# Another order of TensorE's 950 units in a fused talking-heads attention and squared-ReLU FFN

## The chip, the cores and the metric

The kernel runs on one core of one Trainium2 chip. The metric is the time of one execution in device microseconds.

## What is computed

Eight batches of attention with 12 heads, 448 positions and 64 elements a head, in which the heads are mixed before and after the softmax, and then an FFN with a squared ReLU over the 3584 tokens:

```python
scale = 1.0 / np.sqrt(q.shape[-1])
scores = scale * np.matmul(q, k.transpose(0, 1, 3, 2))
scores = np.einsum('bhij,hg->bgij', scores, w_pre)
scores = scores - np.max(scores, axis=-1, keepdims=True)
attn = np.exp(scores)
attn = attn / (np.sum(attn, axis=-1, keepdims=True) + 1e-09)
attn = np.einsum('bhij,hg->bgij', attn, w_post)
x = np.matmul(attn, v)            # (8, 12, 448, 64), as tokens (3584, 768)
h = np.maximum(x @ w_in, 0.0)     # (3584, 2048)
out = h * h @ w_out               # (3584, 768)
```

Inputs and output are float32. The kernel works in bfloat16 with float32 sums in PSUM.

## The kernel before

The whole kernel is a list of tasks that a planner lays out when the program is built. Nothing is decided on the chip: each engine gets a fixed list, and semaphores order the lists against each other.

TensorE's work is cut into units, each a run of matmuls that is issued without a break. The units form ten streams, and within a stream their order is fixed:

- **T** (L841 in batch 0, L847 after): transposes of q and k.
- **QK** (L1087): the scores of one tile of query rows, for two heads a unit or, in the last tile of 64 rows, four. Each score tile is copied to `stage` by ACT or DVE (L486, L487), and SP's DMAs then lay it out anew in `dring` (the relayout, L1134), 10 query rows to a slot, so that heads stand on partitions.
- **pre** (L1162, L1170, L1177): the head mixing before the softmax, two slots of `dring` at a time. ACT takes the exponential into `pring` (L1215), DVE the reciprocal of the sums into `rinv` (L1231), POOL folds it into the second mixing matrix, `wk2s` (L1239), and DVE or POOL multiplies the last columns, `ptail` (L1250).
- **post** (L1287): the head mixing after the softmax, 14 matmuls to a unit, evicted to `a2t` by ACT or DVE.
- **AV** (L1349): attention times values, evicted to `xt`.
- **direct** (L985, L1006, L1028): scores and first mixing of batch 0 without a relayout.
- **F1** (two streams; L1401 in batches 0 and 1, L1427 after): the first FFN product, with ReLU on ACT or DVE (L1460, L1461) and the square on DVE (L1470) into `h2t`.
- **F2** (two streams; L1555, and L1498 for the last two tiles): the second FFN product, evicted to `osb` and stored.

`ORDER`, a string of 950 characters, says from which stream the next unit is taken. A digit is a stream: 0 is T, 1 QK, 2 pre, 3 post, 4 AV, 5 direct, 6 and 7 F1, 8 and 9 F2. Three letters are a stream too, but with another tiling mode of TensorE's array. The units run in modes: *full* (128 x 128), *row* (two halves of 64 rows side by side), *cols* (two halves of 64 columns) and *quad* (four quadrants of 64 x 64). A digit 2 is a pre unit in quadrants, `a` one in row mode and `b` one in column mode; `c` is a QK unit that takes row mode where it could be in quadrants. That choice is there only for the last query tile of a batch, 64 rows; for other QK units `c` and `1` are the same.

```python
STREAM = {"a": 2, "b": 2, "c": 1, **{str(i): i for i in range(10)}}
...
t_qk.alts = {"c": ("row", 2 * 189.2 + 8.0)}
...
t_pre.alts = {"a": ("row", held), "b": ("cols", 2 * 189.2 + 8.0)}
```

The planner goes through `ORDER` in `_Plan.run`, with a cost for each task. It deals the eight PSUM banks out to the units, the oldest free ones first, and gives each task that may run on either of two engines (`FLEX`: most evictions) to the one that would end it first by its costs. So another order also changes which bank a unit gets, which engine evicts it and in which order ACT, DVE and POOL work. `warm_up` puts in extra matmuls (L659) where the plan has long gaps early on.

A unit starts on the chip when its inputs are there and its banks have been evicted. If one waits, all units behind it in TensorE's list wait too.

Of the kernel before, what the change touches and what calls it, by code (L numbers as in the profile page):

```python
# [28 lines left out]
INF = float("inf")  # L29
STREAM = {"a": 2, "b": 2, "c": 1, **{str(i): i for i in range(10)}}  # L30
ORDER = (
    "00c0c0011055cc555555515551551555555155532525b3b350515c2355025aabb5533a00b0a502a3ac33c33b"
    "2144bcb4c2c3b376732263633762272366a773c633336724cc7144cac26377122763676633236c7722c76673"
    "c9cc392239a9338a00381218b44138334200200c27a81a18c1c83338c33662c167c2267731a67276c3336722"
    "2444213773c66613c76721633001672236722712676381183a8223830072830308c3a8c11822393191339c11"
    "932244229c19a393339ca23244224433a6336c37cc7aa006c163a73c72261167373a63362170037224382200"
    "83a18311811912293392239c83338a38c118c3c4222444423361a16a17c373c61a6303072372161267337326"
    "216a7003734b422009cc913191319c381a382228382293393a39c3c931142224441c83c82228c8336136337a"
    "c722006326227337612167337621637100722009c393cc9c3392228c83a182238813c8a3381c8c3342244224"
    "44223761c716363a63731176c006337221762236733700a8381218382229c92239030931931c9c3c931c9222"  # L40
    "4442c83a383c831381224442227637a6c6c731617c6c36337212762236733378212818333822244422933922"
    "29393383683382287637767a6676733864447667766776678766776789989988988999"
)


# [1792 lines left out]
```

## Time and profile before

| | |
|---|---|
| median of 3 runs | 525.28 us (523.45 to 525.76) |
| profiled execution, its own time | 523.65 us |
| its span | 521.9 us |
| PE busy | 507.9 us (97%) |
| ACT busy | 451.9 us (87%) |
| DVE busy | 436.2 us (84%) |
| POOL busy | 209.5 us (40%) |
| chain that ended last | PE 69%, ACT 19%, DMA 5%, DVE 4% |
| granted TensorE clock | 1.00 |

PE is TensorE's matmuls and PEld its weight loads, which overlap them. The span runs from the first to the last instruction; the execution's own time has 1.75 us around it. Busy shares are averages over stages with different limits, and since matmuls are pipelined, a busy PE is not one at its peak. The chain that ended last is followed back from the last instruction, at each step to what released it.

### The profile page before, as it was taken

How to read it: one execution, taken by the hardware profiler on the slowest of the kernel's cores; microseconds unless marked ns; L12 is line 12 of the kernel's file. 1: busy time of each engine (PE TensorE's matmuls, PEld its weight loads, DVE VectorE, ACT ScalarE, POOL GpSimd, SP SyncE). 2: the span in 40 equal slices, each digit the busy share in tenths (PEclk: the TensorE clock that was granted, in tenths of full speed). 3: DMA queues.
4: the chain of work that ended last, by engine and by line, in shares of the span. 5: the costliest groups of instructions: out<-in, count | busy, mean ns of one | idle time of the engine just before them, and what ended most of it. 6: DMA issues, size and time to landing. Idle time of an engine off the chain costs nothing.

```text
span 521.9 us, 22053 instructions
## 1 busy us (share of the span) xinstructions
PE 507.9 (97%) x8925; PEld 318.8 (61%) x8925; DVE 436.2 (84%) x1213; ACT 451.9 (87%) x1286; POOL 209.5 (40%) x413
## 2 busy tenths in 40 slices
PE   7899999999999999999999999999999999999997
PEld 4344677667856665557546565567555665568974
DVE  8799888889999899988998879988998868976530
ACT  5899998999999899989999999988899898996411
POOL 9405545333464374135532377024633341243010
PEclk9999999999999999999999999999999999999999
DMA  9999999756895599647983689446985566642014
GB/s 177 201 197 159 201 175 201 163 118 133 156 181 139 124 168 171 123 104 168 174 161 62 150 166 200 98 90 152 174 131 117 119 151 121 117 87 64 3 24 103
DMA packets 82518, 72.07 MB, mean 138 GB/s; under 512 B 13502, under 2 KB 79662, under 8 KB 82414
## 3 DMA queue, kind: packets, MB, share of 16 engines
q0 software_dynamic: 36480, 32.58, 39.1%
q1 hardware_dynamic: 45514, 37.83, 30.1%
q8 instruction: 73, 1.20, 0.9%
q10 hardware_dynamic: 420, 0.20, 0.2%
q14 instruction: 31, 0.25, 0.1%
HBM read 45.70 MB, written 11.01 MB: 109 GB/s over the span
## 4 chain that ended last, share of the span: by engine, by line
PE 69%; ACT 19%; DMA 5%; DVE 4%; issue 1%; POOL 1%; SPq 1%; ACTq 0%; DVEq 0%
PE ps L1555 24%; PE ps L1427 16%; ACT pring L1215 8%; PE ps L1349 6%; PE ps L1287 5%; PE ps L1087 5%; ACT stage L486 5%; PE ps L1177 4%; ACT a2t L486 3%; PE ps L1498 2%; PE ps L1401 2%; PE ps L1162 2%; DVE stage L487 2%; ACT h1t L1460 2%; DMA dring<-stage 1%
## 5 line engine op out<-in xcount | busy, mean ns | idle before, releaser
L1215 ACT ACTIVATE pring<-ps 128x448 bf16<-128x448 f32 (+1 forms) x368 | 196.8, 568 | 6.4 <-PE ps L1177 4.6
L1239 POOL TENSOR_TENSOR wk2s<-wk2b,rinv 128x120 bf16<-128x120 bf16 x179 | 73.6, 414 | 208.4 <-DVE rinv L1231 207.0
L1555 PE MATMUL ps<-w_out_sb,h2t 64*128 64x384 bf16 x1664 | 151.8, 323 | 0.1
L487 DVE CAST a2t<-ps 128x420 bf16<-128x420 f32 x202 | 126.3, 655 | 11.2 <-PE ps L1287 10.2
L1427 PE MATMUL ps<-xt,w_in_sb 64*128 64x448 bf16 (+2 forms) x1344 | 122.5, 322 | 0.6 <-ACT stage L486 0.2
L486 ACT ACTIVATE stage<-ps 128x448 bf16<-128x448 f32 (+1 forms) x206 | 106.8, 558 | 10.3 <-PE ps L1087 9.2
L1555 PEld LDWEIGHTS ps<-w_out_sb,h2t 64*128 64x128 bf16 x1664 | 79.2, 94 | 49.3 <-issue 1.5
L486 ACT ACTIVATE a2t<-ps 128x420 bf16<-128x420 f32 x158 | 98.3, 673 | 7.8 <-PE ps L1287 7.4
L487 DVE CAST stage<-ps 128x448 bf16<-128x448 f32 (+1 forms) x154 | 92.2, 616 | 10.5 <-PE ps L1087 8.9
L1427 PEld LDWEIGHTS ps<-xt,w_in_sb 64*128 64x128 bf16 x1344 | 62.7, 94 | 40.7 <-PE ps L1177 1.2
L1215 ACT ACTIVATION_READ_ACCUMULATOR pring<-ps 128x1 f32 (+1 forms) x368 | 85.7, 233 | 0.0
L1590 POOL DMA_DIRECT2D out_dram<-osb x52 | 33.6, 652 | 86.9 <-DVE osb L487 34.2
L1287 PEld LDWEIGHTS ps<-wk2s,pring 60*128 60x128 bf16 x2160 | 52.1, 93 | 26.2 <-ACT pring L1215 2.5
L1287 PE MATMUL ps<-wk2s,pring 60*128 60x60 bf16 x2160 | 61.1, 188 | 3.1 <-issue 1.1
L1087 PE MATMUL ps<-qkt 64*128 64x448 bf16 (+1 forms) x360 | 52.9, 354 | 3.1 <-DVE w_out_sb L948 1.3
L1460 ACT ACTIVATE h1t<-ps 128x448 bf16<-128x448 f32 (+2 forms) x92 | 41.2, 459 | 15.5 <-PE ps L1427 12.6
L1470 DVE TENSOR_TENSOR h2t<-h1t 128x448 bf16<-128x448 bf16 (+2 forms) x176 | 50.9, 322 | 1.9 <-ACT h1t L1460 1.7
L1250 DVE TENSOR_TENSOR ptail<-pring,rinv 128x128 bf16<-128x128 bf16 x161 | 48.2, 299 | 1.3
L1461 DVE TENSOR_SCALAR h1t<-ps 128x448 bf16<-128x448 f32 (+2 forms) x84 | 41.0, 489 | 9.4 <-PE ps L1427 6.5
L1231 DVE RECIPROCAL rinv<-sums 128x2 f32<-128x2 f32 x184 | 28.9, 157 | 18.2 <-ACT pring L1215 17.3
L1401 PE MATMUL ps<-xt,w_in_sb 128*128 128x228 bf16 (+1 forms) x384 | 42.5, 260 | 0.0
L1177 PE MATMUL ps<-dring,wk1r 64*64 64x448 bf16 (+1 forms) x540 | 41.2, 363 | 0.3 <-DMA dring<-stage 0.3
(87 smaller groups left out, 596.4 us busy)
## 6 DMA issues: line engine op xcount, KB each, us to landing
dring<-stage SPq DMA_DIRECT2D x308, 105.0 KB
out_dram<-osb POOLq DMA_DIRECT2D x52, 192.0 KB, 3.8
qraw<-in_q_dram POOLq DMA_DIRECT2D x42, 112.0 KB, 5.4
kraw<-in_k_dram POOLq DMA_DIRECT2D x42, 112.0 KB, 5.6
w_in_sb<-in_moe_w_in_dram POOLq DMA_DIRECT2D x8, 384.0 KB, 11.1
vraw<-in_v_dram POOLq DMA_DIRECT2D x24, 128.0 KB, 5.0
w_out_sb<-in_moe_w_out_dram POOLq DMA_DIRECT2D x8, 384.0 KB, 9.0
vraw<-in_v_dram POOLq DMA_DIRECT2D x24, 96.0 KB, 5.7
```

The costliest lines, as they stand in the source:

```text
L486: return eng.activation(o, i_, AF.Copy)
L487: return eng.tensor_copy(o, i_)
L1087: r_ = eng.matmul(ps[o:o + i_, g.banks[x], 0:S], qkt[r0:r0 + 64, pb, p_ % 3, 0, p_ // 3, i0 + w - i_:i0 + w], qkt[r0:r0 + 64, pb, p_ % 3, ...
L1177: r_ = eng.matmul(ps[64 * y:64 * y + 64, gr.banks[x], 0:S], wk1[64 * x:64 * x + 64 - R0 * x, :], dring[64 * x:64 * x + 64 - R0 * x, (g0 + ...
L1215: return eng.activation(pring[0:r1, pr, 0:S], ps[0:r1, gr.banks[x], 0:S], AF.Exp, accum_out=sums[0:r1, g, :], **bias)
L1239: return eng.tensor_tensor(wk2s[:, p0:p0 + n, :], i0.to_broadcast([128, n, PR]), rinv[:, p0:p0 + n, :].to_broadcast([128, n, PR]), ALU.mult)
L1287: r_ = eng.matmul(ps[:, gr.banks[x], o * PR:(o + 1) * PR], p_, w_, start=True, stop=True)
L1401: r_ = eng.matmul(ps[:, g.banks[0], 0:n], w_in_sb[:, ft, t * 128:(t + 1) * 128], xt[:, ft, c0:c1], start=(ft == 0), stop=(ft == NFT - 1))
L1427: r_ = eng.matmul(ps[z * m:(z + 1) * m, g.banks[x], 0:n], w_in_sb[64 * y:64 * y + 64, ft, t:t + m], xt[64 * y:64 * y + 64, ft, c0:c1], sta ...
L1460: return eng.activation(h1t[:, s, 0:n], ps[:, g.banks[x], 0:n], AF.Relu)
L1470: return eng.tensor_tensor(h2t[:, t16, o0:o0 + n], h1t[:, s, 0:n], h1t[:, s, 0:n], ALU.mult)
L1555: r_ = eng.matmul(ps[z * m:(z + 1) * m, g.banks[hh], 0:FH], h2t[64 * y:64 * y + 64, t16, col + z * m:col + (z + 1) * m], w_out_sb[64 * y:6 ...
```

## The change

Only the string `ORDER` is another. It is the result of a search for the mean of four planned executions, three of them with random delays of evictions, relayouts and fetches. Its first line and its last, of 11:

```diff
 ORDER = (
-    "00c0c0011055cc555555515551551555555155555525b3b350515c2355025aabb5533a00b0a502a3ac33c33b"
+    "00c0100c1055155c555551555c5515555555c55a52323523505c5c235502a5aba5532300a0a50a23ac333c3a"
     ...
-    "29393383683382287637767a6676733864447667766776678766776789989988988999"
+    "393383382228836376a677663763736784447677676867866776677679989998899988"
 )
```

The streams give the same 950 units. 544 of the 950 places hold the same character. Most units move by few places; the largest moves are 13 places later (a pre unit) and 10 earlier (an F2 unit).

Three places in TensorE's list, before and now. The first is in batch 1, where the pre units (L1177) need the relayout of the batch's second score tile; L1401 is F1 of batch 0, L1287 post, L1087 QK of the third tile. Before:

```order
L1287 MATMUL ps<-wk2s,pring 128x60 x6
L1287 MATMUL ps<-wk2b,ptail 128x60 x2
L1287 MATMUL ps<-wk2s,pring 128x60 x6
L1401 MATMUL ps<-xt,w_in_sb 128x228 x6
L1087 MATMUL ps<-qkt 128x448 x2
L1401 MATMUL ps<-xt,w_in_sb 128x228 x12
L1177 MATMUL ps<-dring,wk1r 64x448 x8
L1087 MATMUL ps<-qkt 128x448 x2
L1401 MATMUL ps<-xt,w_in_sb 128x228 x24
```

And now:

```order
L1087 MATMUL ps<-qkt 128x448 x4
L1401 MATMUL ps<-xt,w_in_sb 128x228 x18
L1287 MATMUL ps<-wk2s,pring 128x60 x6
L1287 MATMUL ps<-wk2b,ptail 128x60 x2
L1287 MATMUL ps<-wk2s,pring 128x60 x6
L1177 MATMUL ps<-dring,wk1r 64x448 x8
L1401 MATMUL ps<-xt,w_in_sb 128x228 x18
```

One QK unit and F1 units have moved ahead of the two pre units (L1177 x8). From the last QK unit of the second tile to these pre units there are 14 F1 units now for 12, three QK units for two, and as many post and pre units as before.

The second place is in batch 5: pre units (L1177 in quadrants, L1162 in row mode) between F1 units of batch 4 (L1427) and post units (L1287). Before:

```order
L1287 MATMUL ps<-wk2s,pring 128x60 x6
L1177 MATMUL ps<-dring,wk1r 64x448 x4
L1427 MATMUL ps<-xt,w_in_sb 128x448 x12
L1177 MATMUL ps<-dring,wk1r 64x448 x8
L1427 MATMUL ps<-xt,w_in_sb 128x448 x12
```

And now:

```order
L1287 MATMUL ps<-wk2s,pring 128x60 x6
L1162 MATMUL ps<-dring,wk1r 128x448 x4
L1427 MATMUL ps<-xt,w_in_sb 128x448 x12
L1287 MATMUL ps<-wk2s,pring 128x60 x6
L1287 MATMUL ps<-wk2b,ptail 128x60 x2
L1287 MATMUL ps<-wk2s,pring 128x60 x6
L1162 MATMUL ps<-dring,wk1r 128x448 x4
L1427 MATMUL ps<-xt,w_in_sb 128x448 x12
```

The pre units stand singly between post and F1 units, and in row mode, as their neighbours are, where one and then two of them stood in quadrants.

The third place is in batch 7, where two pre units of the second score tile are followed later by their post units; L1087 with 64 partitions is QK in quadrants, L1555 is F2 of batch 6. Before:

```order
L1177 MATMUL ps<-dring,wk1r 64x448 x4
L1087 MATMUL ps<-qkt 64x448 x4
L1177 MATMUL ps<-dring,wk1r 64x448 x4
L1555 MATMUL ps<-w_out_sb,h2t 128x384 x16
L1087 MATMUL ps<-qkt 64x448 x4
L1555 MATMUL ps<-w_out_sb,h2t 128x384 x16
L1287 MATMUL ps<-wk2s,pring 128x60 x6
L1287 MATMUL ps<-wk2b,ptail 128x60 x2
L1287 MATMUL ps<-wk2s,pring 128x60 x12
```

And now:

```order
L1177 MATMUL ps<-dring,wk1r 64x448 x8
L1287 MATMUL ps<-wk2s,pring 128x60 x6
L1287 MATMUL ps<-wk2b,ptail 128x60 x2
L1287 MATMUL ps<-wk2s,pring 128x60 x6
L1555 MATMUL ps<-w_out_sb,h2t 128x384 x16
L1087 MATMUL ps<-qkt 128x448 x2
L1087 MATMUL ps<-qkt 64x448 x2
L1287 MATMUL ps<-wk2s,pring 128x60 x6
L1287 MATMUL ps<-wk2b,ptail 128x60 x2
L1287 MATMUL ps<-wk2s,pring 128x60 x6
L1555 MATMUL ps<-w_out_sb,h2t 128x384 x16
```

The two pre units stand together, a post unit has come in behind them, one QK unit has gone to row mode (two matmuls of 128 partitions and two of 64), and the other one, not in these rows any more, stands behind the post units that follow.

SP's list of DMAs has the same rows in both orders. POOL's list has 16 tail products for 23; DVE has 168 for 161.

More of the change, by code (lines that the diff above doesn't have):

```diff
@@ L31 @@
 ORDER = (
[L32 to L41, printed above, removed]
-    "29393383683382287637767a6676733864447667766776678766776789989988988999"
+    "00c0100c1055155c555551555c5515555555c55a52323523505c5c235502a5aba5532300a0a50a23ac333c3a"
+    "b144b1a4c2c3a367732263733662272366a1736333367244c11741a127763162276377673263117663227763"
+    "1913192239a9338a00381244128318334200200c2728ca1811c833381336621c761226773ca6727613337622"
+    "244421377316663c17672173030c67223662272167638118a382238307302800a382238c3813911c9c3393cc"
+    "9c2244229319a193339c2a3244224433a63c6c371c720a06316ca73373a621367c7a63362170037224382200"
+    "8ccc83c181a932293392239183ac8331813813c422b444423363ac61a7cc7cc63a63003723721612673373a6"
+    "262170037342249a0019c1c913c92238338223811822933933a91cc9c3342224442183182238318163363a7c"
+    "17220063a63a73a736126733762116700722009119111933392228183a38322838c383ca8311813c42244422"
+    "44322637163c7631a6731c76313600722176226733700a833821183822293922c90309cc9311913393c19222"
+    "444238a1833383c18c2244422267613776cc6317163a3637c22762236c733782238c38338122444229392229"
+    "393383382228836376a677663763736784447677676867866776677679989998899988"
 )
```

## The prediction

> **What bounds the kernel now.** I read the page's engine lines first, then the busy time by stretch, then TensorE's own waits, then single instructions in order of time at the places where the order changes.
>
> ```profile
> span 521.9 us, 22053 instructions
> PE 507.9 (97%) x8925; PEld 318.8 (61%) x8925; DVE 436.2 (84%) x1213; ACT 451.9 (87%) x1286; POOL 209.5 (40%) x413
> ```
>
> Busy time by stretch (the stretch and its length; then PE, PEld, DVE, ACT and POOL busy; granted clock, DMA share, GB/s):
>
> ```profile
> 16.00:60.00 44.00, 40.98 (x669) 20.80 (x668) 39.13 (x115) 40.82 (x124) 15.72 (x30) 1.00 1.05 185
> 60.00:486.00 426.00, 423.04 (x7628) 268.24 (x7626) 373.02 (x1014) 392.96 (x1122) 176.50 (x350) 1.00 0.70 139
> 486.00:522.00 36.00, 32.20 (x442) 23.78 (x436) 9.90 (x34) 8.51 (x22) 2.53 (x4) 1.00 0.20 47
> ```
>
> PE is idle for 44.00 − 40.98 = 3.02 us between 16 and 60 us, and for 426.00 − 423.04 = 2.96 us in all the time from 60 to 486 us. The granted clock is 1.00 in every stretch. ACT is next, with 392.96 of 426 us. So TensorE's stream sets the end, and an order can change three things in it: how long a unit takes in the tiling mode that the order gives it, how often the mode changes, and the waits. The idle time that can be seen after the start-up is 3.02 + 2.96 = 5.98 us, so that is about all that a better order could win from waits. The longest waits, the first of them still in the start-up (us in total, times, longest):
>
> ```profile
> PE ps L1087 <- DVE w_out_sb L948: 1.3, 1, 1.3
> PE ps L1287 <- issue: 1.1, 1, 1.1
> PE ps L1287 <- DVE ptail L1250: 0.5, 1, 0.5
> PE ps L1177 <- DMA dring<-stage: 0.3, 1, 0.3
> ```
>
> **Modes and mode changes.** The prices are read from TensorE's instructions in order of time (start us, us, form, count). What a group costs is the time from its start to the start of the next row shown below it; its own length is longer, since matmuls are pipelined.
>
> ```profile
> 96.61 0.55 PE L1162 MATMUL ps<-dring,wk1r 64*128 64x448 bf16 x4
> 96.99 0.58 PE L847 MATMUL ps<-ident,qkt 64*128 64x64 bf16 x28
> ...
> 97.59 1.47 PE L1555 MATMUL ps<-w_out_sb,h2t 64*128 64x384 bf16 x16
> 98.99 0.38 PE L1087 MATMUL ps<-qkt 64*64 64x448 bf16 x4
> 99.21 0.36 PE L1177 MATMUL ps<-dring,wk1r 64*64 64x448 bf16 x4
> ...
> 101.28 0.57 PE L1170 MATMUL ps<-dring,wk1c 124*64 124x448 bf16 x4
> 101.69 0.50 PE L1349 MATMUL ps<-a2t,vraw 128*64 128x220 bf16 x8
> ...
> 227.44 0.35 PE L1087 MATMUL ps<-qkt 64*128 64x448 bf16 x2
> 227.73 0.57 PE L1177 MATMUL ps<-dring,wk1r 64*64 64x448 bf16 x8
> 228.23 1.47 PE L1555 MATMUL ps<-w_out_sb,h2t 64*128 64x384 bf16 x16
> 229.54 0.25 PE L1287 MATMUL ps<-wk2s,pring 60*128 60x60 bf16 x6
> ```
>
> An F2 unit of 16 matmuls takes 229.54 − 228.23 = 1.31 us when a unit of the same row mode follows, and 98.99 − 97.59 = 1.40 us when a quadrant unit follows: a change of mode costs 0.09 us. A pre unit takes 96.99 − 96.61 = 0.38 us in row mode, 101.69 − 101.28 = 0.41 us in column mode (a column unit follows), and in quadrant mode (228.23 − 227.73 − 0.09) / 2 = 0.205 us. A QK unit of a batch's last, 64-row tile takes 99.21 − 98.99 = 0.22 us in quadrant mode. For its row mode, which before does not use, two row pairs bound it: 2 × (227.73 − 227.44 − 0.09) = 0.40 us; a second pair hidden wholly would make it 0.22, so nothing is lost or gained below that, and I take 0.40.
>
> Counted in the two orders (954 units in each, four warm-ups among them), the matmuls of pre go from 112 to 132 at L1162, from 24 to 12 at L1170 and from 540 to 532 at L1177: five row units more, three column units and two quadrant units less. That is 5 × 0.38 − 3 × 0.41 − 2 × 0.205 = +0.26 us. Three QK units go from quadrant to row mode: 3 × (0.40 − 0.22) = +0.54 us. Mode changes go from 286 to 284: −0.18 us. All other units are there in the same number and form. Together TensorE's own work grows by 0.62 us.
>
> **The start-up.** The order now puts two direct units (L1028) between the last two QK units of the first tile, where before waited longest.
>
> ```profile
> 15.74 0.37 PE L1087 MATMUL ps<-qkt 64*128 64x448 bf16 x2 [1.26 <-DVE w_out_sb L948]
> 17.36 2.12 PE L1028 MATMUL ps<-qkt,w_out_sb 128*128 128x448 bf16 x10 [0.34 <-ACT stage L486]
> 15.05 0.98 ACT L486 ACTIVATE stage<-ps 128x448 bf16<-128x448 f32 x2
> 16.76 1.85 ACT L486 ACTIVATE stage<-ps 128x448 bf16<-128x448 f32 x4
> ```
>
> It looks like a gain of up to 1.26 us, but I cost it at nothing. By the kernel's own dealing out of banks the QK unit waited for a PSUM bank that the first of the two evictions at 15.05 gives back about 0.5 us later (the trace names a DVE instruction). In the new order the second of the two direct units takes that bank, the QK unit the next one, and the direct unit after them needs, as before, the bank that the first eviction at 16.76 frees. It started at 17.36, and ACT's list of work is the same up to there, so it starts at 17.36 again. The bounds are 0 and −1.26.
>
> **The relayout at 84 us.** Two pre units of batch 1 wait here for the relayout of its second score tile (the first place shown with the change). First the chain that ended last, then TensorE:
>
> ```profile
> 72.26 0.32 PE ps L1087 x2
> 77.03 7.44 DMA dring<-stage
> 84.51 0.38 PE ps L1177 x4
> ```
>
> ```profile
> 82.59 1.34 PE L1401 MATMUL ps<-xt,w_in_sb 128*128 128x228 bf16 x12
> 83.86 0.38 PE L1177 MATMUL ps<-dring,wk1r 64*64 64x448 bf16 x4
> ```
>
> The tile's last QK unit runs at 72.26, the first pre unit at 83.86, and the second waits until 84.51 for its relayout, 0.3 us. In the new order two F1 units (L1401) and one QK unit more stand in between: (83.86 − 82.59) + 0.20 = 1.47 us more cover, against a wait of 0.3 us. It goes: −0.3. If the relayout lands later too, it stays. SP's list of relayouts is the same, so what each is queued behind does not change; POOL's loads keep their order but for one pair of batch 5 and 6.
>
> **The tail products at 456 us.** Here a post unit waits for DVE (the third place shown with the change):
>
> ```profile
> 455.88 0.62 DVE L487 CAST stage<-ps 64x448 bf16<-64x448 f32 x1
> 456.42 0.28 DVE L1250 TENSOR_TENSOR ptail<-pring,rinv 128x128 bf16<-128x128 bf16 x1
> 456.76 0.26 PE L1287 MATMUL ps<-wk2s,pring 60*128 60x60 bf16 x6 [0.54 <-DVE ptail L1250]
> ```
>
> The tail product (L1250) stood behind a score eviction (0.62 us) of the second quadrant QK unit. In the new order that QK unit comes after the post unit, and the work between the pre unit and its post unit is two F2 units as before, one QK unit and one post unit more. The wait goes: −0.54 us. If DVE takes another eviction in its stead, it stays; the bounds are 0 and −0.54.
>
> **The instruction wait.** The wait of 1.1 us put down to "issue" falls inside one post unit at 57 us. The successions of post, pre and F1 around it have the same forms and counts in both orders, so I leave it. The queue of instructions:
>
> ```profile
> q8 instruction: 73, 1.20, 0.9%
> ```
>
> The Trainium skill, "Runtime: NRT & Kernel Launch", section Instruction fetch mechanics, says that an engine's instructions come in blocks of 256 and that crossing a block is mostly hidden. The 73 transfers, one for some 250 of TensorE's instructions, agree with the blocks; that 1.1 us had no other releaser speaks against "hidden" here. By the rule the wait would be an accident and gone, and the sum 1.1 us lower.
>
> **New waits.** I counted in the orders how much TensorE work stands between each unit after 60 us and the nearest unit whose eviction it needs. Less than 1.25 us of cover have 66 units before and 74 now; between 1.25 and 1.5 us it is 93 and 82. If all 2.96 us of idle time after 60 us belonged to the 66, eight more would cost 0.36 us; if none did, nothing. I take +0.4.
>
> **The sum.** +0.62 − 0.3 − 0.54 + 0.4 = +0.2 us. The profiled execution took 523.65 us (span 521.9 and 1.75 around it), so the same kind of execution would take 523.85. It lies 1.63 us below the median of the runs shown, 525.28; on that median the forecast is 525.5 us. Within 0.5% (2.6 us, about what a measurement of this kernel can tell, with runs from 523.45 to 525.76) is no change.
>
> **Rivals.**
>
> *Most waits go (faster).* An order with more slack against late evictions, relayouts and instructions could take two thirds of the 5.98 us: −4.0 + 0.62 = −3.4, so 521.9 us. For it speaks that two of the waits quoted have more cover. Against it: the issue wait, 1.1 of the 5.98 us, stands where the order gives nothing, and short covers have not become fewer. It needs 2.6 + 0.62 = 3.2 us of waits gone before it shows.
>
> *ACT becomes the bound (slower).* The evictions are dealt out between ACT and DVE again with the new order. ACT gets 162 of the evictions to a2t for 158; DVE loses those four and takes seven tail products from POOL. In batch 6 alone five a2t evictions go from DVE to ACT.
>
> ```profile
> L487 DVE CAST a2t<-ps 128x420 bf16<-128x420 f32 x202 | 126.3, 655 | 11.2 <-PE ps L1287 10.2
> L486 ACT ACTIVATE a2t<-ps 128x420 bf16<-128x420 f32 x158 | 98.3, 673 | 7.8 <-PE ps L1287 7.4
> 380.00:420.00 40.00, 39.85 (x748) 24.35 (x742) 36.20 (x91) 36.84 (x102) 13.58 (x28) 1.00 0.61 123
> 420.00:460.00 40.00, 39.30 (x661) 23.19 (x655) 32.38 (x84) 35.48 (x98) 11.59 (x23) 1.00 0.60 121
> ```
>
> The four are 4 × 0.673 = 2.7 us; the smaller kinds, of which ACT gains some and gives some back, I put at +0.8, together 3.5 us. The five of batch 6 are 3.4 us. ACT has 40.00 − 36.84 + 40.00 − 35.48 = 7.68 us of idle time there, which is why I don't expect it. But its exponentials (L1215) can't go to another engine, and each pair of them holds two PSUM banks. If the 3.5 us came in bursts and TensorE had to wait for all of them, the time would be 525.28 + 0.62 + 3.5 = 529.4 us. It decides from the point where more than some 2 of the 3.5 us fall into bursts. The Trainium skill, "TensorEngine Tiling (Array Packing)", section PSUM Bottleneck, says that tiling speeds up TensorE and not the eviction of PSUM, which may then become the bottleneck; ACT's 392.96 of 426 us agrees that it is near, PE's 423.04 that it is not there yet.
>
> **How the numbers follow.** The forecast of no change has 0.55: the terms known are small and of both signs. The faster rival gets 0.20, the slower one 0.25, as work was added for sure and the waits are only thought to go. The range reaches to the slower rival, 529.5, and a little beyond the faster one, 521.5; the forecast's own range is 523 to 528.
>
> **What would show it.** In the profile after, PE should be busy as before within 1 us, with an idle time of 5 to 6.5 us between 16 and 486 us; L1028 should start its row near 17.4 us again; the wait of L1177 for a relayout near 84 us and that of L1287 for ptail near 456 us should be gone; the issue wait near 57 us should still be there. The forecast is wrong if PE's idle time changes by over 3 us, or if the units between two places of the same kind take longer without idle time.

## The result, and the profile after

The changed kernel takes 525.58 us (median of 20 runs, 524.24 to 528.16), the kernel before 523.42 us (20 runs, 522.16 to 525.76). The ratio is 1.0042 (95% interval 1.0027 to 1.0058): 2.2 us or 0.4% slower, under the 0.5% within which the forecast called it no change. The forecast was 525.5 us.

The profiled execution of the changed kernel took 528.16 us, 4.5 us more than the one of before. The page's engine lines:

```profile
span 526.4 us, 22062 instructions
PE 511.6 (97%) x8925; PEld 317.5 (60%) x8925; DVE 437.4 (83%) x1212; ACT 455.1 (86%) x1294; POOL 207.2 (39%) x406
```

Busy time by stretch, columns as in the prediction:

```profile
16.00:60.00 44.00, 40.62 (x661) 20.51 (x660) 40.12 (x119) 40.14 (x122) 15.72 (x30) 1.00 1.06 185
60.00:490.00 430.00, 426.05 (x7621) 266.32 (x7621) 375.02 (x1015) 396.37 (x1130) 174.13 (x343) 1.00 0.69 138
490.00:527.00 37.00, 32.76 (x454) 24.34 (x450) 9.11 (x33) 8.98 (x23) 2.52 (x4) 1.00 0.19 46
```

PE idles for 44.00 − 40.62 = 3.38 us between 16 and 60 us, and for 430.00 − 426.05 = 3.95 us from 60 to 490: 7.33 us, where before had 5.98. Its waits (us in total, times, longest) and the two places of the prediction, TensorE's instructions in order of time:

```profile
PE ps L1287 <- issue: 2.1, 2, 1.9
PE ps L1555 <- issue: 1.0, 1, 1.0
PE ps L1087 <- DVE h1t L1461: 0.3, 1, 0.3
```

```profile
17.33 2.12 PE L1028 MATMUL ps<-qkt,w_out_sb 128*128 128x448 bf16 x10
...
86.93 0.57 PE L1177 MATMUL ps<-dring,wk1r 64*64 64x448 bf16 x8
...
457.54 1.46 PE L1555 MATMUL ps<-w_out_sb,h2t 64*128 64x384 bf16 x16
458.84 0.66 PE L1087 MATMUL ps<-qkt 64*128 64x448 bf16 x4
459.43 0.26 PE L1287 MATMUL ps<-wk2s,pring 60*128 60x60 bf16 x6
```

The start-up ends at 17.33 us (17.36 before). The pair of pre units at 86.93 no longer waits for its relayout, nor does the post unit at 459.43 for ptail. The issue wait is still inside the same post unit, 1.88 us long instead of 1.1, and something follows it (TensorE's rows, then the stretches 58 to 66 us of the changed kernel and, last, of before):

```profile
58.84 0.20 PE L1287 MATMUL ps<-wk2s,pring 60*128 60x60 bf16 x1 [1.88 <-issue]
58.97 1.58 PE L1401 MATMUL ps<-xt,w_in_sb 128*128 128x220 bf16 x12
60.48 0.96 PE L1177 MATMUL ps<-dring,wk1r 64*64 64x448 bf16 x8
...
58.00:62.00 4.00, 3.16 (x25) 1.95 (x26) 1.60 (x7) 2.34 (x6) 1.28 (x2) 0.73 1.27 220
62.00:66.00 4.00, 4.00 (x54) 2.45 (x54) 2.89 (x11) 3.28 (x13) 1.02 (x3) 0.84 1.18 217
```

```profile
58.00:62.00 4.00, 3.90 (x54) 2.83 (x54) 2.69 (x12) 3.56 (x12) 1.72 (x3) 1.00 1.20 206
```

One microsecond after the wait the granted clock is halved for 3.4 us (0.73 and 0.84 on average in two stretches of 4 us). Most of the 3.7 us by which PE's busy time grew comes from there, where the same matmuls last longer, and from a second such stretch near 12 us, in the start-up, which cost nothing (the direct units start on time). The rest, 1.2 us, is the order's (see "Where the rest goes"). The wait (0.8 us longer) and the half clock (1.7 us lost) make up 2.5 of the 4.5 us by which the two profiled executions differ, and the next sections ask whether the order is to blame for them.

To follow the rest, I compared when TensorE starts a unit ahead of which the same units have run. A number is how many us the kernel is later there than before; the columns are named by the time in before's profile.

| kernel profiled | 52 | 67 to 73 | 138 | 200 | 253 | 316 | 365 | 392 | 422 | 459 | 512 |
|---|---|---|---|---|---|---|---|---|---|---|---|
| changed kernel | -0.2 | 2.5 | 1.9 | 3.2 | 3.9 | 3.9 | 3.9 | 4.4 | 4.7 | 4.7 | 4.6 |
| old head, new rest | -0.2 | 2.2 | 2.0 | 2.1 | 2.8 | 2.7 | 2.8 | 3.6 | 3.8 | 3.8 | 3.7 |
| new head, old rest | -0.2 | 0.4 | 0.0 | 0.2 | 0.3 | -0.1 | -0.1 | -0.1 | -0.1 | -0.4 | -0.4 |
| two places new | 1.0 | 1.4 | 1.5 | 2.0 | 2.0 | 1.6 | 1.6 | 1.6 | 1.6 | 1.7 | 2.4 |
| before, warm-up cut | 0.6 | -0.5 | -0.6 | -0.4 | -0.4 | -0.7 | -0.8 | -0.8 | -0.5 | -0.9 | -0.9 |
| changed, warm-up cut | -0.1 | -0.8 | -1.4 | -1.2 | -0.4 | -0.4 | -0.4 | 1.4 | 1.6 | 1.6 | 1.5 |
| middle new | 1.1 | 0.1 | -0.1 | 0.5 | 1.7 | 1.6 | 2.3 | 3.6 | 3.7 | 3.6 | 3.6 |
| end new | 1.0 | 1.2 | 1.5 | 1.7 | 1.7 | 1.3 | 1.4 | 2.7 | 3.0 | 3.0 | 2.9 |
| first copy moved, warm-up cut | -0.2 | -0.8 | -1.4 | -1.3 | -0.6 | -0.6 | -0.6 | 0.6 | 1.2 | 1.2 | 1.1 |

### The profile page after: what moved, and what is told of

It is laid out like the page before. It is cut to its first block, busy times and chain, and to the rows that moved or that the text cites. A ratio compares the mean times of both kernels' runs of the same rounds, so it can differ in the third digit from the quotient of the medians.

```text
span 526.4 us, 22062 instructions
## 1 busy us (share of the span) xinstructions
PE 511.6 (97%) x8925; PEld 317.5 (60%) x8925; DVE 437.4 (83%) x1212; ACT 455.1 (86%) x1294; POOL 207.2 (39%) x406
## 4 chain that ended last, share of the span: by engine, by line
PE 70%; ACT 17%; DVE 5%; DMA 4%; issue 2%; POOL 1%; SPq 0%; ACTq 0%
PE ps L1555 24%; PE ps L1427 15%; ACT pring L1215 7%; PE ps L1349 6%; PE ps L1287 6%; PE ps L1177 5%; PE ps L1087 5%; ACT stage L486 5%; PE ps L1401 4%; ACT a2t L486 3%; DMA kraw<-in_k_dram 2%; PE ps L1162 2%; PE ps L1498 2%; DMA wall<-in_w_pre_dram 1%; DVE stage L487 1%
## 5 line engine op out<-in xcount | busy, mean ns | idle before, releaser
L1555 PE MATMUL ps<-w_out_sb,h2t 64*128 64x384 bf16 x1664 | 152.1, 323 | 1.1 <-issue 1.0
L1427 PE MATMUL ps<-xt,w_in_sb 64*128 64x448 bf16 (+2 forms) x1344 | 122.0, 322 | 0.4 <-ACT a2t L486 0.2
L486 ACT ACTIVATE a2t<-ps 128x420 bf16<-128x420 f32 x162 | 101.2, 679 | 9.8 <-PE ps L1287 9.2
L1555 PEld LDWEIGHTS ps<-w_out_sb,h2t 64*128 64x128 bf16 x1664 | 79.0, 94 | 49.3 <-issue 3.2
L1427 PEld LDWEIGHTS ps<-xt,w_in_sb 64*128 64x128 bf16 x1344 | 62.1, 94 | 42.3 <-PE ps L1087 1.1
L1287 PEld LDWEIGHTS ps<-wk2s,pring 60*128 60x128 bf16 x2160 | 51.9, 93 | 29.8 <-issue 4.5
L1287 PE MATMUL ps<-wk2s,pring 60*128 60x60 bf16 x2160 | 61.4, 188 | 3.6 <-issue 2.1
L1087 PE MATMUL ps<-qkt 64*128 64x448 bf16 (+1 forms) x360 | 52.7, 356 | 1.6 <-ACT qkt L486 1.2
L1250 DVE TENSOR_TENSOR ptail<-pring,rinv 128x128 bf16<-128x128 bf16 x168 | 50.8, 302 | 1.4
L1401 PE MATMUL ps<-xt,w_in_sb 128*128 128x228 bf16 (+1 forms) x384 | 43.4, 263 | 0.2
L1177 PE MATMUL ps<-dring,wk1r 64*64 64x448 bf16 (+1 forms) x532 | 41.9, 368 | 0.4 <-ACT pring L1215 0.2
## 6 DMA issues: line engine op xcount, KB each, us to landing
w_in_sb<-in_moe_w_in_dram POOLq DMA_DIRECT2D x8, 384.0 KB, 11.5
```

What stands on the lines that cost most here:

```text
L486: return eng.activation(o, i_, AF.Copy)
L1087: r_ = eng.matmul(ps[o:o + i_, g.banks[x], 0:S], qkt[r0:r0 + 64, pb, p_ % 3, 0, p_ // 3, i0 + w - i_:i0 + w], qkt[r0:r0 + 64, pb, p_ % 3, ...
L1177: r_ = eng.matmul(ps[64 * y:64 * y + 64, gr.banks[x], 0:S], wk1[64 * x:64 * x + 64 - R0 * x, :], dring[64 * x:64 * x + 64 - R0 * x, (g0 + ...
L1250: return eng.tensor_tensor(ptail[:, p0 // 2, :, :], pring[:, p0:p0 + n, 0:PJ], rinv[:, p0:p0 + n, :].to_broadcast([128, n, PJ]), ALU.mult)
L1287: r_ = eng.matmul(ps[:, gr.banks[x], o * PR:(o + 1) * PR], p_, w_, start=True, stop=True)
L1401: r_ = eng.matmul(ps[:, g.banks[0], 0:n], w_in_sb[:, ft, t * 128:(t + 1) * 128], xt[:, ft, c0:c1], start=(ft == 0), stop=(ft == NFT - 1))
```

## The experiments

Medians are of 12 runs each, with the ratio to the kernel before on the same chip. Kernels of different experiments ran on different chips, so they are better compared by these ratios than by their times.

**Which part of the order.** Theory: the new order causes the long wait at 57 us and what follows it. Rivals: these come by chance, and the loss lies in the rest of the order. In the first kernel the old order's 146 first places (up to about 72 us) stand ahead of the new order's rest, in the second the other way round.

```diff
-ORDER = NEW
+ORDER = OLD[:146] + NEW[146:]
```

> The new order with the first 146 of its 950 units in the old order (up to about 72 us; TensorE has done the same units by then in both). Theory 1, instruction delivery: the time was lost at the block of instructions near 57 us (a wait of 1.9 us against 1.1, then the TensorE clock halved for 3.4 us) and at the one near 161 us (1.0 us). Then the loss up to 72 us, 2.3 us in the profiles, is gone and the wait near 161 us is left: about +1.5 us on the kernel before (+0.3%), clock 1.00. Theory 2, spread: the 0.6 us of added TensorE work and many small waits for evictions all along cost it. Then the head gives back only its share, some 0.3 us, and the kernel stays at +1.9 us (+0.36%), with no instruction wait more than in the kernel before.

```diff
-ORDER = OLD
+ORDER = NEW[:146] + OLD[146:]
```

> The old order with the first 146 units in the new order. Theory 1: the longer instruction wait near 57 us is there and in some of the executions the halved clock after it: +0.8 to +2.5 us on the kernel before (+0.15 to +0.5%); no instruction wait near 161 us. Theory 2: the head has only its share of the added work, +0.1 us by the counts of modes (+0.0%), and stays within 0.1% of the kernel before.

The old head with the new rest takes 526.29 us (ratio 1.0035, 1.0009 to 1.0061), the new head with the old rest 524.24 us (1.0012, 0.9990 to 1.0033). The wait in the post unit, in the first and in the second:

```profile
58.82 0.18 PE L1287 MATMUL ps<-wk2s,pring 60*128 60x60 bf16 x1 [1.88 <-issue]
```

```profile
58.06 0.20 PE L1287 MATMUL ps<-wk2s,pring 60*128 60x60 bf16 x1 [1.10 <-issue]
```

The old head had the long wait, with the half clock behind it, and the new head the short one. So the first theory falls: the wait is in both orders, and its length is an execution's chance. What the new order loses, it loses after 73 us: in the table the first kernel goes on from 2.2 to 3.7, the second from 0.4 to −0.4.

**Modes.** The changed order, but each pre and QK unit in the mode that the old order gave it; that makes 303 mode changes for 284.

```diff
-"...2a1c..."   (the new order's choice of a, b, c or 1, 2)
+"...a21c..."   (each unit's choice from the old order)
```

> The new order of units, but each pre and QK unit in the tiling mode that it had in the old order. Counted in the program: five row pre units, three row QK units less, three column and two quadrant pre units more (-0.8 us by the rows of before), and 303 mode changes instead of 284 (+1.7 us at 0.09 us each): +0.9 us on the new order, so about +3.1 us on the kernel before (+0.6%). If a mode change costs nothing on the path, as it would if TensorE's waits hid it, it is -0.8 us on the new order, +1.4 us on the kernel before (+0.27%).

526.40 us (1.0051, 1.0028 to 1.0074), 0.8 us above the changed kernel, where +0.9 was expected. But the count behind that figure is wrong. From matmul to matmul, without the warm-up units, the mode changes 282 times in the trace of before, 286 times in that of the changed kernel and 299 times here: 13 more and not 19, because a QK unit in row mode changes the mode twice inside itself (see the term on modes below). At 0.09 us that is 1.2 us, less 0.8 us for the shorter units: +0.4 us. The intervals overlap, so the time doesn't tell the two counts apart, and the new places were not tried with as few changes and the old modes. One row of its TensorE is used below:

```profile
380.02 0.36 PE L1087 MATMUL ps<-qkt 64*128 64x448 bf16 x2 [0.80 <-DVE h1t L1461]
```

**The two waits alone.** The old order with only the two places from which the prediction took gains, around 84 and 456 us.

```diff
-ORDER = OLD
+ORDER = OLD[:146] + NEW[146:179] + OLD[179:841] + NEW[841:873] + OLD[873:]
```

> The old order with only two stretches of the new one: units 146 to 178 (the relayout place near 84 us) and 841 to 872 (the tail-product place near 456 us). In the profiles the new order won 0.5 us at the first and 0.8 us at the second. If these gains belong to the places, the kernel is 1.0 to 1.3 us faster than the kernel before (-0.2 to -0.25%), and both waits are gone from its profile. If they were chance of one execution, or if the waits move to the next unit, it is within 0.1%.

525.21 us (1.0026, 1.0003 to 1.0048): slower, where a gain was expected. Both waits go in its profile. But the half clock appears at another time (clock in the stretch 44 to 48 us, which is 1.00 in before):

```profile
44.00:48.00 4.00, 3.92 (x56) 2.21 (x58) 3.67 (x9) 3.94 (x12) 0.38 (x1) 0.59 1.14 184
```

Without that first 1.0 us (52 us column), the profile still ends 1.3 us late. Around 456 us 0.8 us is lost ahead of the wait that goes: two QK units of 64 rows take 0.59 us each, as they are in row mode now, and a pair of pre units takes 0.2 us more. Another 0.7 us is lost after it, 0.38 of it in a wait of TensorE for ACT's exponentials. So what one place gains is given back near it.

**The wait for instructions.** The wait lies at the 1729th or 1730th of TensorE's instructions (matmuls, weight loads, semaphores) in all the profiles that show it, always where a block of 256 begins (1729 = 6 × 256 + 193; the 161 us wait of the changed kernel is at 5313 = 20 × 256 + 193). The block's transfer in queue q8 began 4.8 us after the crossing before it in before's profile, and 6.0 us in that of the changed kernel, with the DMA engines full (share 1.2 from 56 to 58 us). If a block's border is the cause, moving the border must move the wait. The warm-up matmuls are cut in four, so that 102 more instructions stand ahead:

```diff
-for _ in range(n):
-    r_ = eng.matmul(ps[0:128, g.banks[0], 0:S], warm[:, 0:128], warm[:, :], ...)
+for x in range(4 * n):
+    r_ = eng.matmul(ps[0:128, g.banks[0], x % 4 * 112:x % 4 * 112 + 112], warm[:, 0:128], warm[:, 0:112], ...)
```

> The order is that of the kernel before. Only the warm-up matmuls are cut up: each of the 17 of 448 columns becomes four of 112, so that 102 more instructions (matmuls and their weight loads) stand ahead of the rest of TensorE's list. DVE's, ACT's, POOL's and SP's lists stay as they are. Theory A (the wait of 1.1 to 1.9 us at 57 us is a wait for the next 256 of TensorE's instructions, late there because its transfer shares the DMA engines with the second FFN matrix; by chance it is followed by 3.4 us at half clock): the wait inside that post unit goes; the boundary now lies some 3 us earlier and later in the list, and a wait there is shorter than 0.5 us. The time is 1.1 us below before, 522.5 for 523.6 us. Rival B (the wait belongs to this place in the list, to a semaphore or a queue that the profile does not show): it stays at 57 us with 1 us or more, and the time is that of before within 0.5 us.

> The same cut of the warm-up matmuls in the changed kernel, whose order stays as it is. If the changed kernel lost its time to waits for instructions (the 1.9 us at 57 us, the half clock behind them, the 1.0 us at 161 us), these waits move with the boundary or go, and the time falls to that of the kernel before with the same cut, within 0.5 us of it. If the loss lies in many small waits for evictions and in the modes of the units, which this edit does not touch, it falls by some 1.1 us, as much as the kernel before does, and stays 1.5 to 2 us above that one.

Before with the cut: 522.65 us (0.9980, 0.9961 to 0.9999). The changed kernel with the cut: 525.24 us (1.0025, 1.0005 to 1.0044). The only issue wait left over 0.5 us is in the first, in another unit, again at a border (5 × 256 + 193):

```profile
48.21 0.43 PE L1349 MATMUL ps<-a2t,vraw 128*64 128x220 bf16 x6 [0.70 <-issue]
```

So theory A holds for the place: the wait belongs to the block's border. That the second FFN matrix's loads are what delays the transfer was not tested. The cut takes about 0.2% from either kernel (1.0000 to 0.9980; 1.0042 to 1.0025, with intervals that overlap), so it explains nothing of the difference between them. Before with the cut warm-up is also the one version that beats both kernels, if barely: its interval ends at 0.9999.

**Where the rest goes.** The old order with one stretch of the new one.

```diff
-ORDER = OLD
+ORDER = OLD[:286] + NEW[286:616] + OLD[616:]
```

> The order of the kernel before, with the changed kernel's places 286 to 615 in its middle (137 to 315 us); both orders have taken the same units at both ends. Theory C (the loss is a sum of small waits and mode work spread over the order): this third costs what the profile of the kernel with the old head and the new rest lost in it, +0.7 us, so 524.3 us for 523.6. Rival D (any other order of this kind deals banks and engines anew for all that follows, and loses some 1.5 us wherever it is put in): 1.5 us or more, 525.1 us, most of it after 315 us, where the order is the old one again.

```diff
-ORDER = OLD
+ORDER = OLD[:616] + NEW[616:]
```

> The order of the kernel before up to place 615, and the changed kernel's from there (315 us to the end). Theory C: +1.0 us, 524.6 us for 523.6, with the losses near 376, 400 and 444 to 453 us that the profile of the kernel with the old head and the new rest shows, and a gain of 0.7 us at 457 us. Rival D: 1.5 us or more. If this third gains nothing and loses nothing (within 0.3 us), the loss lies in the middle alone or in how the parts act on each other.

525.29 us (1.0037, 1.0015 to 1.0059) and 525.05 us (1.0028, 1.0001 to 1.0055). Both parts cost, together more than the whole order, and the medians do not tell theory C from D. The profiles do better. In the table, the kernels with the new order between 138 and 253 us lose 0.8 to 2.0 us there (1.0 of the 2.0 is the changed kernel's second issue wait), those with the old one 0.1 to 0.5; between 365 and 392 us it is 0.5 to 1.8 against 0.0, but for the kernel with the new middle, which loses 1.3 us there in the old order (its two waits there, 0.59 and 0.50 us, are for evictions by DVE that no load holds up).

How much of the loss is waiting can be read from the same 7900 matmuls in each profile, from the unit at 67 us of before to the one at 512, all at full clock (stretch, length, PE, PEld, DVE, ACT and POOL busy, clock, DMA share, GB/s). Before, and before with the cut warm-up:

```profile
67.00:512.00 445.00, 442.24 (x7900) 283.33 (x7898) 376.82 (x1027) 393.00 (x1118) 176.59 (x349) 1.00 0.66 132
66.54:511.10 444.56, 442.16 (x7900) 283.35 (x7898) 376.93 (x1027) 392.63 (x1118) 176.02 (x349) 1.00 0.66 132
```

The changed kernel, the same with the cut warm-up, and the last kernel of these experiments, in which the first copy is moved:

```profile
69.43:516.54 447.11, 443.46 (x7900) 281.25 (x7898) 377.49 (x1027) 395.51 (x1125) 174.21 (x342) 1.00 0.65 130
66.09:513.52 447.43, 443.37 (x7900) 280.19 (x7898) 377.12 (x1027) 396.26 (x1125) 174.89 (x342) 1.00 0.65 131
66.08:513.10 447.02, 443.74 (x7900) 280.59 (x7898) 377.21 (x1026) 396.85 (x1126) 175.28 (x342) 1.00 0.66 132
```

In all three profiles with the old order here (the third is that of the new head), PE is busy for 441.8 to 442.2 us and idle for 2.4 to 2.8; in all six with the changed order (these three, the old head, and two of the moved copy below) it is busy for 443.4 to 443.9 us and idle for 2.9 to 4.1. On average the order costs 2.4 us here: TensorE works 1.5 us longer and waits 0.9 us longer. (A matmul's end in the profile is modelled and lies some 0.15 us behind the start of the next, so a shorter wait is hidden under it and counts as work.) So the larger part of the loss is no wait at all; it is taken up with the prediction's term on modes.

The waits at the two places are of one kind. First the end, in the changed kernel with the cut warm-up: DVE, then TensorE.

```profile
374.48 0.62 DVE L487 CAST stage<-ps 128x448 bf16<-128x448 f32 x1
376.96 0.62 DVE L487 COPY qkt<-kraw 128x896 bf16<-128x896 bf16 x1 [1.86 <-DMA kraw<-in_k_dram]
377.49 0.15 DVE L1231 RECIPROCAL rinv<-sums 128x2 f32<-128x2 f32 x1
377.56 0.60 DVE L1461 TENSOR_SCALAR h1t<-ps 128x448 bf16<-128x448 f32 x1
```

```profile
376.30 0.36 PE L1087 MATMUL ps<-qkt 64*128 64x448 bf16 x2
378.23 0.36 PE L1087 MATMUL ps<-qkt 64*128 64x448 bf16 x2 [1.57 <-DVE h1t L1461]
```

DVE's next job is a copy of k for batch 7, and it waits 1.86 us for that load. Behind it in DVE's list stands the eviction of an F1 unit (`h1t`), and the QK unit at 378.23 needs that bank. In the old order this copy is ACT's and the QK unit's banks are freed by other evictions; the copy ran there at 376.25 us without a wait:

```profile
376.25 0.94 ACT L486 ACTIVATE qkt<-kraw 128x896 bf16<-128x896 bf16 x1
```

The last load of that copy was issued at 368.0 us here and at 368.1 us in before. From issue to landing it took 8.94 us here (the chain of waits) and 5.4 us in before (its loads from 366 to 371 us). This goes with the order and is not one execution's chance: it is 7.1 to 8.9 us in the eight profiles with the new end that show it, 5.0 to 5.4 us in four with the old end, and 6.5 us with the new middle. POOL issues this load 3.2 us after the load of q three loads ahead of it in the new end, and 4.4 us after it in the old; whether that is why it lands later was not tested.

```profile
368.00 8.94 DMA kraw<-in_k_dram
```

```profile
DMA to landing us min/median/max: 5.4/5.4/5.4
```

Every profile with the new order's end shows this copy on DVE. In those so far TensorE's wait behind it varies: 0.29 us in the changed kernel, 0.6 with the old head, 0.80 with the old modes, 1.17 in the kernel with the new end, 1.57 here.

At 210 us it is the copy of v (`vodd`) that waits, here in the kernel with the new middle, DVE then TensorE:

```profile
207.74 0.27 DVE L1250 TENSOR_TENSOR ptail<-pring,rinv 128x128 bf16<-128x128 bf16 x1
209.00 0.35 DVE L487 COPY vodd<-vraw 64x768 bf16<-64x768 bf16 x1 [0.98 <-DMA vraw<-in_v_dram]
```

```profile
213.02 0.26 PE L1287 MATMUL ps<-wk2s,pring 60*128 60x60 bf16 x6 [0.77 <-DVE h1t L1461]
```

With the new order here, a wait of the copy for 0.60, 0.68 or 0.98 us goes with one of the post unit for 0.41, 0.48 or 0.77 us behind it; where the copy waits 0.2 us or not at all, the post unit does not wait. In the old order this copy never waits here.

**Moving the copy.** If DVE's place for the copy is the cause, the wait must go when the copy stands behind the eviction. The planner is told that the loads land later, first those of heads 4 to 7:

```diff
-t.end = max(t.end, now + DMA_END[t.dma[0]])
+t.end = max(t.end, now + DMA_END[t.dma[0]] + 4000 * t.name.startswith("ldqk7_1_1"))
```

> The changed kernel with its order as it is. Only the planner is told that the two loads of k for batch 7, heads 4 to 7, land 4 us later than it assumed, so that DVE's copy of them (kraw to qkt) stands just behind the eviction of the F1 unit (h1t, L1461) that it stood ahead of; TensorE's list is the same, and DVE's, ACT's and POOL's differ in some rows behind this place. Theory E (DVE works in the order of its list: the copy waits for its load, the eviction behind it waits with it, and a QK unit near 376 to 381 us waits for the bank, 0.3 to 1.6 us by execution): the wait of L1087 for DVE h1t is gone, and the time falls by 0.9 us, the mean of the waits seen in five profiles with this order (0.3, 0.6, 0.8, 1.6, 1.2), to 524.7 us for 525.6. Rival (the wait only moves to the next unit, or to the transposes that need the copy): the time stays within 0.3 us.

> The same, and the warm-up matmuls cut into four as well, so that both named waits of the changed kernel (for instructions at 57 us, for h1t at 376 us) are taken away. Theory: 524.3 us, 0.9 us below the changed kernel with the cut alone (525.24). What is left between it and the kernel before with the same cut (522.65) is the mode work and small waits, 0.6 to 1.7 us. If the named waits were all of the loss, it comes to 522.7 us.

> The order of the kernel before up to place 615 and the changed kernel's from there, with the cut warm-up and the copy behind the eviction. Theory E: the last third cost 1.6 us in its profile without the two edits, 1.3 of them at 376 us; so it now costs 0.2 to 0.3 us over the kernel before with the cut (522.65): 522.9 us. Rival D (any splice deals banks and engines anew and costs 1.5 us wherever it is): 524.2 us or more.

525.55 us (1.0037, 1.0014 to 1.0061), 524.40 us (1.0013, 0.9995 to 1.0030) and 523.49 us (0.9998, 0.9975 to 1.0021). These three tested less than they were meant to: the copy in the traces is that of heads 0 to 3, and this edit moves the next one. In the first, the load took 7.1 us, the shortest time with the new end, and nothing waits; in the second, the copy waits as ever (DVE, then TensorE), and so it does in the third:

```profile
377.15 0.62 DVE L487 COPY qkt<-kraw 128x896 bf16<-128x896 bf16 x1 [1.14 <-DMA kraw<-in_k_dram]
```

```profile
378.42 0.36 PE L1087 MATMUL ps<-qkt 64*128 64x448 bf16 x2 [0.84 <-DVE h1t L1461]
```

So the first time, equal to the changed kernel's, says nothing against the theory, and the second, which is the figure expected, nothing for it. The third is 0.8 us above before with the same cut (522.65; by the ratios 0.9998 and 0.9980, with intervals that overlap), and its profile loses 1.0 us between 365 and 392 us: between theory E and rival D. Then the right copy, with the cut warm-up:

```diff
+t.end = max(t.end, now + DMA_END[t.dma[0]] + 3000 * t.name.startswith("ldqk7_0_1"))
```

> The changed kernel with the cut warm-up, and the right copy moved this time. The copy that DVE waits with near 376 us is the one ahead of a reciprocal and an F1 eviction (h1t, L1461), right behind a score eviction: k of batch 7, heads 0 to 3. The edit before had moved that of heads 4 to 7, and the wait of L1087 for DVE h1t was still there in two of its three profiles (0.8 and 0.9 us). Now the planner takes the loads of heads 0 to 3 to land 3 us later; DVE's copy goes behind six more of its instructions, and the eviction that stood behind it goes to ACT. TensorE's list is the same. Theory E: the wait of L1087 for DVE h1t near 376 us is gone, TensorE loses under 0.2 us there against the kernel before (1.7 us in the changed kernel with the cut alone, 0.8 and 0.9 with the wrong copy), and the time is 524.3 us, 0.9 us below the 525.24 of the changed kernel with the cut. Rival (the wait moves to the next score unit, two instructions on, whose bank is now evicted behind the copy): a wait of 0.5 us or more stays between 375 and 382 us, and the time is 525.2 us.

525.41 us (1.0037, 1.0016 to 1.0058): no gain on 525.24 (1.0025, 1.0005 to 1.0044), though the 0.9 us expected are no more than such an interval reaches to either side. The wait near 376 us is gone as theory E says. But 8 us later the copy of heads 4 to 7, which has stayed ahead of another F1 eviction, waits in its turn (DVE, then TensorE):

```profile
378.37 0.61 DVE L487 COPY qkt<-kraw 128x896 bf16<-128x896 bf16 x1
...
384.27 0.62 DVE L487 COPY qkt<-kraw 128x896 bf16<-128x896 bf16 x1 [1.29 <-DMA kraw<-in_k_dram]
...
385.61 0.61 DVE L1461 TENSOR_SCALAR h1t<-ps 128x448 bf16<-128x448 f32 x1
```

```profile
386.27 0.57 PE L1177 MATMUL ps<-dring,wk1r 64*64 64x448 bf16 x8 [0.47 <-DVE h1t L1461]
```

Theory E is right on what makes TensorE wait, and wrong that one edit takes the time back: the rival holds, with the wait moved further than it said. Moving both copies at once was not tried, so the price of the mechanism is read from profiles and is not shown in the time. In the six profiles with the changed order such waits come to 0.3 to 2.0 us, 0.8 us on average.

## Why the prediction was right, and which terms were wrong

The forecast of no change within 0.5% held, and the figure is 0.1 us off; but that closeness is luck: the sum, +0.2 us, stood on a median of 3 runs, 1.9 us above the one measured later, and against that one the order costs 2.2 us. Two terms of the sum were too small, the modes and the new waits.

- **Start-up, 0:** right. The direct units start at 17.33 us, and the units that follow them up to 30 us are 0.02 to 0.04 us early.
- **Relayout at 84 us, −0.3:** right. The wait is gone, and TensorE gains 0.4 to 0.5 us at this place.
- **Tail products at 456 us, −0.54:** the wait is gone, but from 422 to 459 us the changed kernel gains only 0.1 us, because two of the three QK units in row mode stand there. With the old modes, where they are in quadrants, the same stretch gains 0.55 us. The wait was also partly that execution's: in two more profiles with the old order there it was 0.2 us, in a third 0.46.
- **The issue wait, unchanged:** right that both orders have it, and that it is not the order's. The rule of the Trainium skill, "Runtime: NRT & Kernel Launch", section Instruction fetch mechanics, that a crossing is mostly hidden, holds for nearly all of the 73 blocks; for the one at 57 us it failed in eight of nine profiles without the cut (1.1 to 1.9 us). The half clock behind it was not foreseen.
- **Modes, +0.62:** too small, because the mode changes were miscounted. The sum took a QK unit in row mode for four matmuls in one mode. It is a row pair followed by a quadrant pair, so each of the three brings two changes of its own. TensorE has six quadrant matmuls of L1087 fewer and not twelve (before, then the changed kernel):

```profile
L1087 PE MATMUL ps<-qkt 64*64 64x448 bf16 x84 | 7.5, 362 | 0.0
L1087 PE MATMUL ps<-qkt 64*64 64x448 bf16 x78 | 7.3, 360 | 0.0
```

The unit takes 459.43 − 458.84 = 0.59 us (in the rows of the result above), and all 25 in the profiles take 0.591 or 0.592 us, where the sum had 0.40. So there are four mode changes more than before, not two fewer, and the term comes to 0.62 + 3 × 0.19 = 1.2 us. TensorE's busy time, 1.5 us up between 67 and 512 us at full clock, agrees with that, with 0.3 us left open. The kernel with the old modes is busy no shorter, 443.7 us, as its 13 mode changes more outweigh its shorter units. No run took these three units alone back to quadrants.
- **New waits, +0.4:** too small as well. After 67 us the sum had the idle time go down by 0.3 + 0.54 − 0.4 = 0.44 us, and on average it went up by 0.9. I had counted TensorE's work between a unit and the eviction it needs. I did not look at what stands ahead of that eviction on its own engine, and there stands a copy that waits for a load. The waits behind such copies, 0.8 us on average, are the largest part of the new ones. A wait of 0.41 us for DVE's eviction to `a2t` near 275 us stands in all six profiles, one of 0.34 us for ACT's to `h1t` near 267 us in five; the rest is smaller, but for the changed kernel's 1.0 us for instructions.

The marks set for the profile: idle time between 16 and 490 us is 7.33 us for a forecast of 5 to 6.5, which the one execution's long wait explains; PE's busy time is 3.7 us up for a forecast of 1, for the larger part by the half clock; the two waits are gone as said. But one of the signs of being wrong that the prediction named did come, units that take longer without idle time: the three QK units.

Of the rivals, the faster one (most waits go) is out, since waits were exchanged and not removed. The slower one was right in direction and wrong in engine. ACT does get the a2t evictions that it named:

```profile
L486 ACT ACTIVATE a2t<-ps 128x420 bf16<-128x420 f32 x162 | 101.2, 679 | 9.8 <-PE ps L1287 9.2
L487 DVE CAST a2t<-ps 128x420 bf16<-128x420 f32 x198 | 125.1, 658 | 10.6 <-PE ps L1287 9.3
```

But after 60 us no wait of TensorE for ACT is longer than 0.34 us in the changed kernel. In the six profiles with the changed order every wait over 0.4 us after 67 us, but for the one for instructions, is a wait for DVE, and the longest of them come while DVE itself is idle, behind a copy that waits for its load.

## What to carry to other kernels

An order that is planned against costs fixes more than the order: it deals out banks and engines, and a job that waits for a load can come to stand ahead of an eviction, where its wait becomes TensorE's. So judge such a change by what stands ahead of each eviction on its engine, and give the jobs that depend on loads slack by how long loads really took in the trace, the longest and not the median. Count mode changes from matmul to matmul in the trace and not from unit to unit in the plan: a unit can change the mode inside. And profile a change of 0.4% more than once before explaining it: here over half of the difference between two profiled executions was chance, and no one edit gave the rest back. What held in every profile was found by comparing the same matmuls, between the same two units, and splitting the time into work and waits.

## What the hardware showed that was not expected

TensorE's clock was halved for stretches of 3.413 us each in a kernel that otherwise runs at full clock. They came 1 us after a wait of 1.9 us (two profiles), in three profiles near 45 us with only 0.8 to 0.9 us of idle time in the 4 us ahead, and in three in the start-up, at 11.5 to 14 us; waits of 1.1 to 1.6 us elsewhere had none behind them, so the trigger stays open. The Trainium skill, "TensorE: Matmul & The Clock Gate", section "Part 1: The HAM clock gate", says that activity is judged in free-running windows of 3413 ns, and that the clock falls after an idle one. The length agrees with these rows, and windows that run free would make the fall a matter of chance; if an idle window is one that is idle as a whole, the rows do not agree, with at most 2.0 us idle in the 4 us ahead of any of the eight. Executions whose mean clock is below 0.9985 (7 of 20 of the changed kernel, 13 of 35 of before in one comparison) have medians 1.7 and 1.0 us above the others. The others of the two kernels, on two chips, have medians of 525.23 and 523.18 us, 2.0 us apart, so the order's cost is not the clock's.
